# Last batch of a fused attention and convolution kernel: inverse transform interleaved with the previous batch's output projection, and one output DMA per chunk of 128 rows

## The chip, the cores and the metric

One NeuronCore of one Trainium2 chip runs the whole program. The metric is the device time of one execution in microseconds (us). Most executions of one kernel agree within about 1% here. Ratios in this document are the mean time of one kernel's fast runs over the mean time of the other's fast runs of the same rounds on the same chip, so they are not quite the ratios of the medians that are quoted beside them. An interval in brackets is a 95% interval. Some executions fall in a slower state; on one core, as here, a run counts as slow when it is over 1.5% above the fastest of its kernel.

A "profile" is one execution recorded by the hardware profiler. It gives each instruction's start and length, what it waited for, and each DMA packet. The engines are PE (TensorE), DVE (VectorE), ACT (ScalarE), POOL (GpSimd) and SP (SyncE). SyncE computes nothing here; it issues output DMAs. "SPq" and "ACTq" are the instructions with which SyncE and ScalarE issue a DMA; an issue goes to the queue of its engine. A matmul leaves its result in a PSUM tile, and an "eviction" is the copy from there to SBUF by ScalarE or VectorE, from where a DMA stores it.

## The reference

For 8 batches of 8 heads, 576 positions and 64 channels:

```python
kv  = einsum('bhsd,bhse->bhde', k, v)
out = einsum('bhsd,bhde->bhse', q, kv)
x   = rms_norm(out) * g_norm            # to (8, 576, 512)
x1, x2, x3 = split(x @ w_proj)          # 512 columns each
y   = x1 * irfft(rfft(x2) * rfft(filter)) * x3      # over the 576 positions
return y @ w_out                        # float32, (8, 576, 512)
```

The output of one batch is 576 rows of 512 float32, 1.18 MB.

## The kernel before

The batches are software-pipelined. While batch b's gates and transforms run, batch b+1's attention runs beside them, and batch b-1's output projection (`outp`) is done just before batch b's inverse transform. Only the last batch has nothing to overlap with, so it has a routine of its own, `last`.

The rows come out in nine blocks of 64. Block x holds rows 192*(x//3) + x%3 + 3*i, for i = 0..63. So rows of one block lie three rows apart in memory, and 128 consecutive columns of `yg` (one chunk) are two such blocks.

```python
def o_rows(b, *blks):
    t0 = [SB * (x // 3) + x % 3 for x in blks]
    two = [[(t0[1] - t0[0]) * DM, 2]] if len(t0) == 2 else []
    return bass.AP(..., offset=out.offset + (b * S + t0[0]) * DM, ap=[[3 * DM, 64]] + two + [[1, DM]])

def inv(b, dcs):                        # one quarter (dc) of the inverse
    ...                                 # 6 matmuls of 288 columns into PSUM
    nc.scalar.copy(out=os_, in_=p_[1])  # os has one buffer
    nc.vector.tensor_add(out=u[...], in0=p_[0], in1=os_)
    nc.vector.tensor_sub(out=u[...], in0=p_[0][...], in1=os_[...])
    nc.vector.tensor_mul(out=st[b]['yg'][:, d2], in0=u, in1=g13[:, d2])

def last(b):
    po = [ps_tile("ps_out") for _ in range(3)]
    def part(dc):                       # the share of one dc in all five chunks
        for c in range(4):
            nc.tensor.matmul(po[c // 2][:, c % 2], st[b]['yg'][:, dc, c * P:(c + 1) * P], wo[:, dc], **kw)
        for i, y in enumerate((yt[0], st[b]['yg'])):   # block 8 of batches b-1 and b
            nc.tensor.matmul(po[2][64 * i:64 * i + 64, 0], y[:, dc, 4 * P:S], wo[:, dc], **kw)
    for dc in range(NDC):
        inv(b, (dc,))
        if dc:
            part(dc - 1)
    part(NDC - 1)
    for c in range(NSC):                # evict and store, chunk by chunk
        ...
        if c % 2:
            nc.vector.tensor_copy(out=ot[:, 0], in_=src)
        else:
            nc.scalar.copy(out=ot[:, 0], in_=src)
        for i in range(2):              # two DMAs of 64 rows, two queues
            bb, blk = (b, 2 * c + i) if c < 4 else (b - 1 + i, NR - 1)
            (nc.scalar if i else nc.sync).dma_start(out=o_rows(bb, blk), in_=ot[64 * i:64 * i + 64, 0])

# the loop's end, batch b
if b:
    for c0 in (0, 2, 4):
        outp(b - 1, c0)                 # all of batch b-1's projection first
if not nxt:
    last(b)
```

Of the kernel before, what the change touches and what calls it, by code (L numbers as in the profile page):

```python
# [9 lines left out]
FP32 = mybir.dt.float32  # L10
# [5 lines left out]
P = 128  # L16
# [4 lines left out]
def kernel(  # L21
# [16 lines left out]
    nc = tc.nc  # L38
    B, H, S, D = q.shape
    DM = H * D  # L40
    D3 = 3 * DM
    assert (B, H, S, D) == (8, 8, 576, 64)
    SB = S // 3
    TH = S // 2
    NDC = DM // P
    NSC = 5
# [6 lines left out]
    work = ctx.enter_context(tc.tile_pool(name="work", bufs=1))  # L53
    psp = ctx.enter_context(tc.tile_pool(name="psp", bufs=4, space=bass.MemoryType.PSUM))

    def ps_tile(name):
        return psp.tile([P, 2, 512], FP32, name=name, tag="ps")
# [4 lines left out]
    NR = S // 64  # L62
# [63 lines left out]
    wo = consts.tile([P, NDC, DM], BF16)  # L126
# [14 lines left out]
    for r0, n, a, na, base, step in ((0, 64, 0, 2, 0, 2), (64, 64, 0, 2, 1, SB - 1), (0, 32, 2, 1, SB + 1, 1)):  # L141
        nc.gpsimd.dma_start(out=fa[r0:r0 + n, a:a + na], in_=bass.AP(
            tensor=moe_filter_fft.tensor, offset=moe_filter_fft.offset + base * DM,
            ap=[[3 * DM, n], [step * DM, na], [1, DM]]))
# [20 lines left out]
    for c, tag in enumerate(("x", "Y", "g13")):  # L165
# [15 lines left out]
        tensor=g_norm.tensor, offset=g_norm.offset, ap=[[0, 2], [1, D]]))  # L181
# [31 lines left out]
    x_t, st = {}, {}  # L213
# [82 lines left out]
    def fold(b, jp):  # L296
        s = st[b]
        if jp == 0:
            s['ab'] = work.tile([P, NDC, 2 * SB], BF16, name="ab", tag="ab")
            s['rr'] = work.tile([P, NDC, SB], BF16, name="rr", tag="rr")  # L300
        j2 = slice(2 * jp, 2 * jp + 2)
        x3 = s['x'][:, j2].rearrange("p j (m r) -> p j m r", m=3)
        d_ = work.tile([P, 2, 2, SB], BF16, name="d_", tag="d_")
        nc.vector.tensor_sub(out=d_, in0=x3[:, :, 0:3:2], in1=x3[:, :, 1:2].to_broadcast([P, 2, 2, SB]))
        t_ = work.tile([P, 2, SB], BF16, name="x01", tag="x01")
        nc.vector.tensor_add(out=t_, in0=x3[:, :, 0], in1=x3[:, :, 2])
        r_ = work.tile([P, 2, SB], BF16, name="x012", tag="x012")
        nc.vector.tensor_add(out=r_, in0=t_, in1=x3[:, :, 1])
        hb = SB // 2
        for half, op in ((0, nc.vector.tensor_add), (1, nc.vector.tensor_sub)):  # L310
            op(out=s['rr'][:, j2, half * hb:(half + 1) * hb], in0=r_[:, :, 0:hb], in1=r_[:, :, SB - 1:hb - 1:-1])
            op(out=s['ab'][:, j2, half * SB:(half + 1) * SB], in0=d_[:, :, 0], in1=d_[:, :, 1, ::-1])  # L312
# [127 lines left out]
    def inv(b, dcs):  # L440

        Y, g13 = st[b]['Y'], st[b]['g13']
        if dcs[0] == 0:
            st[b]['yg'] = work.tile([P, NDC, S], BF16, name="yg", tag="yg", bufs=3)
        m = len(dcs)
        if m == 2:
            po, pe = ps_tile("ps_invo"), ps_tile("ps_inve")
            p_ = (pe[:, :, 0:TH], po[:, :, 0:TH])
        else:
            pp = ps_tile("ps_inv")  # L450
            p_ = (pp[:, 0:1, 0:TH], pp[:, 1:2, 0:TH])
        for h in (1, 0):
            for i, dc in enumerate(dcs):
                for g in range(3):
                    n = N1 if g == 0 else P
                    nc.tensor.matmul(p_[h][:, i], Y[:n, 2 * g + h, dc * P:(dc + 1) * P], IV[:n, 2 * g + h],  # L456
                                     start=(g == 0), stop=(g == 2))
        os_ = work.tile([P, 2, TH], FP32, name="os", tag="os")[:, 0:m]
        nc.scalar.copy(out=os_, in_=p_[1])  # L459
        u = work.tile([P, 2, S], BF16, name="u", tag="u", bufs=2)[:, 0:m]  # L460
        nc.vector.tensor_add(out=u[:, :, 0:TH], in0=p_[0], in1=os_)
        nc.vector.tensor_sub(out=u[:, :, TH:S], in0=p_[0][:, :, ::-1], in1=os_[:, :, ::-1])  # L462
        d2 = slice(dcs[0], dcs[0] + m)
        nc.vector.tensor_mul(out=st[b]['yg'][:, d2], in0=u, in1=g13[:, d2])

    yt = {}

    def o_rows(b, *blks):
        t0 = [SB * (x // 3) + x % 3 for x in blks]
        two = [[(t0[1] - t0[0]) * DM, 2]] if len(t0) == 2 else []  # L470
        return bass.AP(tensor=out.tensor, offset=out.offset + (b * S + t0[0]) * DM, ap=[[3 * DM, 64]] + two + [[1, DM]])

    def outp(b, c0):
        if c0 < 4 or b % 2:
            yg = yt[b % 2] = st[b]['yg']
            pp = ps_tile("ps_out")
            if c0 < 4:
                for cc in range(2):
                    c = c0 + cc
                    for dc in range(NDC):  # L480
                        nc.tensor.matmul(pp[:, cc], yg[:, dc, c * P:(c + 1) * P], wo[:, dc], start=(dc == 0), stop=(dc == NDC - 1))  # L481
            else:
                for dc in range(NDC):
                    for i in range(2):
                        nc.tensor.matmul(pp[64 * i:64 * i + 64, 0], yt[i][:, dc, 4 * P:S], wo[:, dc],
                                         start=(dc == 0), stop=(dc == NDC - 1))
            ot = work.tile([P, 2, DM], FP32, name="ot", tag="ot", bufs=3)
            n = 2 if c0 < 4 else 1
            if c0 == 0:
                nc.vector.tensor_copy(out=ot, in_=pp)  # L490
            else:
                nc.scalar.copy(out=ot[:, 0:n], in_=pp[:, 0:n])  # L492
            for i in range(2):
                if n == 2:
                    nc.sync.dma_start(out=o_rows(b, 2 * c0 + i, 2 * c0 + 2 + i), in_=ot[64 * i:64 * i + 64])
                else:
                    nc.sync.dma_start(out=o_rows(b - 1 + i, NR - 1), in_=ot[64 * i:64 * i + 64, 0])

    def last(b):

        po = [ps_tile("ps_out") for _ in range(3)]

        def part(dc):
            kw = dict(start=(dc == 0), stop=(dc == NDC - 1))
            for c in range(4):
                nc.tensor.matmul(po[c // 2][:, c % 2], st[b]['yg'][:, dc, c * P:(c + 1) * P], wo[:, dc], **kw)
            for i, y in enumerate((yt[0], st[b]['yg'])):
                nc.tensor.matmul(po[2][64 * i:64 * i + 64, 0], y[:, dc, 4 * P:S], wo[:, dc], **kw)

        for dc in range(NDC):  # L510
            inv(b, (dc,))
            if dc:
                part(dc - 1)
        part(NDC - 1)
        for c in range(NSC):
            ot = work.tile([P, 2, DM], FP32, name="ot", tag="ot", bufs=3) if c < 3 else \
                work.tile([P, 2, 2, DM], FP32, name="ot_", tag="tpw", bufs=2)[:, 0]
            src = po[c // 2][:, c % 2]
            if c % 2:
                nc.vector.tensor_copy(out=ot[:, 0], in_=src)  # L520
            else:
                nc.scalar.copy(out=ot[:, 0], in_=src)
            for i in range(2):
                bb, blk = (b, 2 * c + i) if c < 4 else (b - 1 + i, NR - 1)
                (nc.scalar if i else nc.sync).dma_start(out=o_rows(bb, blk), in_=ot[64 * i:64 * i + 64, 0])


    qtr(0)
# [9 lines left out]
    for b in range(B):  # L538
        nxt = b + 1 < B
        proj2(b)  # L540
        if b == 0:
            fold_filter()
            proj13(0, 0)
            proj13(0, 1)
            gen_h(1)
            gen_h(0)
            qtr(1)
            gen_h(2)
            kv(1)
        elif nxt:  # L550
            kv(b + 1)
            qtr(b + 1)
        if b + 2 < B:
            load_kv(b + 2, (0, 8))
            load_q(b + 2)
        if b == 0:
            att_o(1, 0)
            fft(0, 1)
            att_o(1, 1)
            att_r(1, 0)  # L560
            fft(0, 0)
            att_r(1, 1)
            att_x(1, 0)
            fold(1, 0)
            att_o(1, 2)
            proj13(0, 2)
            att_o(1, 3)
            att_r(1, 2)
            fft(0, 2)
            att_r(1, 3)  # L570
            att_x(1, 1)
            fold(1, 1)
            proj13(0, 3)
        for dc in range(NDC) if b else ():
            if dc < 3:
                fft(b, (1, 0, 2)[dc])
            if nxt:
                att_o(b + 1, dc)
            proj13(b, dc)
            if nxt:  # L580
                att_r(b + 1, dc)
                if dc % 2:
                    att_x(b + 1, dc // 2)
                    fold(b + 1, dc // 2)
        if b:
            for c0 in (0, 2, 4):
                outp(b - 1, c0)
            del st[b - 1]
        if not nxt:
            last(b)  # L590
            continue
        for dp in (0, 2):
            inv(b, (dp, dp + 1))

# [29 lines left out]
```

## Time and profile before

| what | value | from |
|---|---|---|
| time, median of the first three runs | 255.63 us (254.88 to 257.65) | runs |
| span of the profiled run | 252.9 us (that run took 255.09) | profile |
| PE busy over the span | 88% | profile, part 1 |
| end of the last gate projection (L432) | 230.90 us | chain of waits |
| last eviction ends | 249.09 us | timeline |
| span ends, counted from the last gate projection | 22.0 us | 252.9 - 230.9 |

From run to run the point where the last gate projection ends moves by some 2 us either way, though the program up to there is the same. The stretch after it, the **tail**, repeats far better: in the three kernels with the old order (before, e2, e11) the first eviction starts 13.26 us into it each time. So from here on I count times in profiles from the end of the last gate projection. In the chain of waits of the kernel before, that is the end of this piece (start, length, what):

```profile
226.87 4.03 PE ps_x L432 x32
```

A second view cuts the tail into stretches. Its columns are the stretch, its length, then for PE, PE's weight loads, DVE, ACT and POOL the busy us and instruction count, then the granted clock, the mean busy share of the 16 DMA engines, and the GB/s:

```profile
230.90:240.90 10.00, 8.73 (x50) 4.15 (x48) 5.57 (x11) 2.11 (x4) 0.00 (x0) 1.00 0.37 105
240.90:245.00 4.10, 3.31 (x17) 1.26 (x15) 1.76 (x5) 0.99 (x2) 0.00 (x0) 1.00 0.00 0
245.00:253.00 8.00, 0.00 (x0) 0.00 (x0) 1.16 (x2) 1.17 (x2) 0.00 (x0) 0.64 0.57 164
```

In the first 10 us PE idles for 1.3 us, and in the last 8 us it does nothing at all: there the output is evicted and stored.

### The profile page before, as it was taken

What the parts mean: (1) busy time and instruction counts of PE and PEld (TensorE: products, weight loads), DVE (VectorE), ACT (ScalarE), POOL (GpSimd) and SP (SyncE); (2) the same over time, 40 slices, a digit from 0 to 9 for tenths busy, and PEclk for the clock granted to TensorE, in tenths of its full rate; (3) what the DMA queues carried; (4) which work ended last, traced back from release to release, by engine and by line L of the source; (5) the groups of instructions that cost most, each with busy time, mean ns of one, the idle gap of its engine ahead of it and who ended that gap; (6) DMA issues with size and microseconds to landing.
All of it is one profiled execution on the core that took longest, in us unless ns stands there. A gap on an engine that the chain in (4) does not pass through costs nothing.

```text
span 252.9 us, 4825 instructions
## 1 busy us (share of the span) xinstructions
PE 222.7 (88%) x1927; PEld 132.3 (52%) x1927; DVE 195.1 (77%) x354; ACT 153.3 (61%) x230; POOL 89.7 (35%) x101
## 2 busy tenths in 40 slices
PE   0377997787999999999999999999999999999760
PEld 0343453453665566655665566547664765466420
DVE  6669747799797969795998699769987997696441
ACT  2764336991689468945894689566956696522311
POOL 7964970670491049102920292003300330042000
PEclk9999999999999999999999999999999999999995
DMA  6999999993297529752994199420023003400506
GB/s 69 167 202 251 202 196 191 193 136 43 19 180 85 158 26 181 87 160 54 160 119 115 56 162 118 117 95 1 0 66 103 3 0 75 135 0 3 166 20 187
DMA packets 45623, 27.17 MB, mean 107 GB/s; under 512 B 22274, under 2 KB 40706, under 8 KB 45602
## 3 DMA queue, kind: packets, MB, share of 16 engines
q0 software_dynamic: 40160, 17.44, 55.1%
q1 hardware_dynamic: 5042, 8.78, 12.2%
q10 hardware_dynamic: 400, 0.66, 0.7%
q8 instruction: 15, 0.25, 0.4%
q14 instruction: 6, 0.05, 0.1%
HBM read 33.69 MB, written 9.44 MB: 171 GB/s over the span
## 4 chain that ended last, share of the span: by engine, by line
PE 69%; ACT 13%; DVE 9%; issue 3%; DMA 2%; POOL 2%; ACTq 1%; POOLq 0%; DVEq 0%
PE ps_x L432 19%; PE ps_out L481 10%; PE ps_x L383 6%; PE ps_invo L456 4%; PE ps_inve L456 4%; PE ps_qT L248 3%; ACT lr L284 3%; PE ps_x L389 3%; PE ps_x L374 3%; PE ps_r L283 2%; ACT osb L272 2%; ACT sq L267 2%; DMA vm<-in_v_dram 2%; PE ps_kv L223 2%; PE ps_o L266 2%
## 5 line engine op out<-in xcount | busy, mean ns | idle before, releaser
L432 PE MATMUL ps_x<-x,wp 128*128 128x288 bf16 x512 | 67.8, 286 | 0.7
L415 POOL TENSOR_TENSOR Y<-tpw 128x1024 bf16<-128x1024 f32 (+1 forms) x16 | 37.9, 2366 | 66.3 <-PE ps_r L283 40.7
L432 PEld LDWEIGHTS <-wp 128*128 128x128 bf16 x512 | 49.7, 98 | 15.5 <-issue 2.9
L70 POOL DMA_DIRECT2D km<-in_k_dram x9 | 7.9, 878 | 64.4 <-PE ps_qT L248 58.4
L267 ACT ACTIVATE sq<-ps_o 128x576 bf16<-128x576 f32 x32 | 20.7, 653 | 13.4 <-PE ps_o L266 13.4
L438 DVE TENSOR_TENSOR g<-ps_x,x 128x576 bf16<-128x576 f32 x32 | 24.0, 751 | 5.3 <-PE ps_x L432 3.5
L284 ACT ACTIVATE lr<-ps_r,bias_eps 128x576 f32<-128x576 f32 x32 | 23.5, 751 | 6.9 <-PE ps_r L283 6.9
L436 ACT CAST x<-ps_x 128x576 bf16<-128x576 f32 x32 | 20.7, 648 | 8.4 <-PE ps_x L432 8.4
L481 PE MATMUL ps_out<-wo,yg 128*128 128x512 bf16 x112 | 25.3, 379 | 0.0
L253 DVE COPY qT<-ps_qT 128x512 bf16<-128x512 bf16 (+1 forms) x32 | 13.4, 453 | 14.7 <-PE ps_qT L248 14.6
L456 PEld LDWEIGHTS <-Y 128*128 128x128 bf16 (+1 forms) x192 | 18.2, 97 | 9.2 <-DVE Y L421 1.8
L413 DVE TENSOR_TENSOR tpw<-ps_X,HH 128x1024 f32<-128x1024 f32 (+1 forms) x16 | 19.5, 1219 | 3.9 <-PE ps_X L411 3.3
L272 ACT ACTIVATE osb<-ps_o,g_col 128x576 bf16<-128x576 f32 x28 | 20.9, 746 | 0.0
L248 PE MATMUL ps_qT<-ident,qb 128*64 128x128 bf16 x288 | 12.3, 232 | 9.3 <-DMA qb<-in_q_dram 8.7
L459 ACT COPY os<-ps_invo 128x576 f32<-128x576 f32 x14 | 9.0, 640 | 18.0 <-DVE u L462 15.3
L414 DVE TENSOR_TENSOR tpw<-ps_X,HH 128x1024 f32<-128x1024 f32 (+1 forms) x16 | 19.4, 1213 | 0.0
L287 ACT ACTIVATE rstd<-lr 128x1152 bf16<-128x1152 f32 x16 | 18.6, 1164 | 0.4
L383 PE MATMUL ps_x<-wp,ab 128*128 128x512 bf16 x64 | 16.9, 404 | 1.3 <-DVE ab L312 1.3
L481 PEld LDWEIGHTS <-yg 128*128 128x128 bf16 x112 | 11.0, 98 | 11.9
L492 ACT COPY ot<-ps_out 128x1024 f32<-128x1024 f32 (+1 forms) x10 | 8.8, 885 | 12.9 <-PE ps_out L481 12.9
L266 PE MATMUL ps_o<-qT,kvblk 128*128 128x288 bf16 x64 | 13.8, 304 | 2.9 <-ACT kvblk L234 1.9
L248 PEld LDWEIGHTS <-qb 128*64 128x64 bf16 x288 | 9.6, 117 | 12.3 <-issue 12.3
(166 smaller groups left out, 396.6 us busy)
## 6 DMA issues: line engine op xcount, KB each, us to landing
out_dram<-ot SPq DMA_DIRECT2D x28, 256.0 KB, 3.6
qb<-in_q_dram POOLq DMA_DIRECT2D x16, 288.0 KB, 7.0
km<-in_k_dram POOLq DMA_DIRECT2D x7, 512.0 KB, 6.1
vm<-in_v_dram POOLq DMA_DIRECT2D x7, 512.0 KB, 8.2
wp<-in_moe_w_proj_dram POOLq DMA_DIRECT2D x3, 512.0 KB, 10.1
out_dram<-ot SPq DMA_DIRECT2D x9, 128.0 KB, 3.0
km<-in_k_dram POOLq DMA_DIRECT2D x2, 256.0 KB, 5.5
kt<-in_k_dram POOLq DMA_DIRECT2D x8, 64.0 KB, 5.7
```

The lines of the kernel that those rows point to most:

```text
L248: mm = nc.tensor.transpose(tp[64 * hp:64 * hp + 64, bank, i * P:(i + 1) * P], qb[b % 2][:, 2 * jj + hp, c * D:(c + 1) * D], ident)
L267: nc.scalar.activation(out=s['sq'][:, j].rearrange("p (a b) -> p a b", a=2), in_=op[:, :, 0:TH], func=AF.Square)
L272: nc.scalar.activation(out=o_, in_=op[:, :, 0:TH], func=AF.Copy, scale=g_col)
L284: nc.scalar.activation(out=s['lr'][:, j % 2].rearrange("p (a b) -> p a b", a=2), in_=r2[:, :, 0:TH], func=AF.Ln, scale=1.0 / D, bias=bias_eps)
L383: nc.tensor.matmul(pp[:, h], ab[:, j, h * SB:h * SB + P], wp[:, j, DM:2 * DM], start=(j == 0), stop=(j == NDC - 1))
L413: nc.vector.tensor_mul(out=t_[:n, 0], in0=xp[:n], in1=HH[:n, g, 1:3])
L415: nc.gpsimd.tensor_add(out=Y[:n, 2 * g:2 * g + 2], in0=t_[:n, :, 0], in1=t_[:n, :, 1])
L432: nc.tensor.matmul(pp[:, h, 0:TH], w_, x[:, j, h * TH:(h + 1) * TH], start=(j == 0), stop=(j == NDC - 1))
L436: nc.scalar.copy(out=x1, in_=pp[:, :, 0:TH])
L438: nc.vector.tensor_mul(out=st[b]['g13'][:, dc].rearrange("p (a b) -> p a b", a=2), in0=pp[:, :, 0:TH], in1=x1)
L456: nc.tensor.matmul(p_[h][:, i], Y[:n, 2 * g + h, dc * P:(dc + 1) * P], IV[:n, 2 * g + h], start=(g == 0), stop=(g == 2))
L481: nc.tensor.matmul(pp[:, cc], yg[:, dc, c * P:(c + 1) * P], wo[:, dc], start=(dc == 0), stop=(dc == NDC - 1))
```

## The change

The intent is threefold. Batch 6's projection is split in two and laid between the quarters of batch 7's inverse, so that TensorE has work while the other engines prepare `yg`. Each chunk of 128 rows then gets a PSUM tile of its own, and ScalarE and VectorE evict chunks side by side. And each chunk leaves in one DMA of 256 KB on SyncE, where two of 128 KB went out on two queues.

```diff
-    def outp(b, c0):
+    def outp(b, c0, ev=None):
 ...
+    def out1(b, c, ev, q1):
+        yg = st[b]['yg']
+        pp = ps_tile("ps_out")
+        for dc in range(NDC):
+            ...                        # 4 matmuls, or 8 half-width ones for chunk 4
+        ev(out=ot[:, 0], in_=pp[:, 0])
+        t0 = [x * S + SB * (y // 3) + y % 3 for x, y in (((b, 2 * c), (b, 2 * c + 1)) if c < 4 else ((b - 1, NR - 1), (b, NR - 1)))]
+        q1.dma_start(out=bass.AP(tensor=out.tensor, offset=out.offset + t0[0] * DM,
+                                 ap=[[(t0[1] - t0[0]) * DM, 2], [3 * DM, 64], [1, DM]]), in_=ot[:, 0])
+
     def last(b):
-        po = [ps_tile("ps_out") for _ in range(3)]
-        ...                            # part() and the evictions, above
         for dc in range(NDC):
             inv(b, (dc,))
-            if dc:
-                part(dc - 1)
+            if dc < 2:
+                outp(b - 1, 2 * dc, nc.scalar.copy)
+        act, dve = nc.scalar.copy, nc.vector.tensor_copy
+        for c, ev in ((4, act), (0, dve), (1, act), (2, act), (3, dve)):
+            out1(b, c, ev, nc.sync)
 ...
+        if not nxt:
+            last(b)
+            continue
         if b:
             for c0 in (0, 2, 4):
                 outp(b - 1, c0)
             del st[b - 1]
-        if not nxt:
-            last(b)
-            continue
```

The store's destination is two blocks of 64 rows of 512, with 2 outermost.

## The prediction

> **What bounds the kernel now.** I read the page first: PE is busy 88% of the span, so the body of the kernel is TensorE's. The change leaves the body alone: the comparison of instruction orders shows the same 3856 TensorE rows, and differences only after the last gate projection (L432). So what counts is the last 22 us, and there I read the chain of waits from 230 us on, pieces with start, length and what ran.
>
> ```profile
> 230.90 3.47 PE ps_out L481 x16
> 234.39 1.01 ACT ot L492
> ...
> 243.00 0.47 DVE yg L464
> 243.47 0.05 issue
> 243.52 0.62 PE ps_out L506 x2
> 244.14 0.02 issue
> 244.16 0.59 ACT ot L522
> 244.76 0.02 issue
> 244.78 0.70 DVE ot L520
> 245.48 0.02 issue
> 245.50 0.69 ACTq L525
> ```
>
> Three stretches are to be seen. TensorE first does batch 6's whole output projection (16 matmuls, 3.47 us) ahead of the last inverse. Then the inverse runs a ladder: a copy on ScalarE, two VectorE operations, the product yg, with TensorE waiting; the last yg ends at 243.47. Then five evictions pass ScalarE and VectorE one after the other, because ScalarE also issues DMAs that wait for VectorE's copy (the "ACTq" piece); the last eviction ends at 249.09, and 3.8 us later the span ends, with its last DMA. Next come the DMA view of the last 8.4 us, and that of the first 12 us, where SyncE's queue q1 carries only the load of g_col:
>
> ```profile
> DMA packets 800, 1.31 MB, mean 156 GB/s; under 512 B 160, under 2 KB 160, under 8 KB 800
> q1 hardware_dynamic: 400, 0.66, 32.3%
> q10 hardware_dynamic: 400, 0.66, 22.3%
> ```
>
> ```profile
> q1 hardware_dynamic: 130, 0.00, 0.5%
> ```
>
> The last batch leaves as ten DMAs of 64 rows: 640 packets of 2 KB and 160 small ones, 16 for each DMA. The small ones are the completions, one from each of 16 engines. But g_col's load (128 elements of 4 bytes, its source described as 2 x 64) made 130 packets: 128 plus **two** completions. It ran on two engines. For this change that is the weightiest line of the profile.
>
> **What the Trainium skill says.** "DMA: Bandwidth & Descriptors", section "Why a DMA increments its semaphore by 16 and not by 1": a DMA's engine count is the largest number up to 16 that divides the size of the slowest dimension of both its access patterns, and only those engines write a completion. The trace agrees: 160 completions for ten DMAs with 64 outermost, 2 for the one with 2 outermost. The same page, "Rules for kernel authors": an outermost dimension under 16 confines the whole DMA to at most that many engines. The same page, "Specifications": some 27 GiB/s for each engine. The trace's shortest 2 KB packets take 81 to 84 ns, 24 GB/s, a little less. The same page, "Issuing engines are not separate DMA queues": SyncE and ScalarE share the engines, so moving all issues to SyncE costs issue time only; the old tail fits, with q1 and q10 moving equal bytes in one stretch.
>
> **The change part by part.** *Interleaving.* Counts stay: 24 inverse matmuls of some 0.123 us (6 take 0.74 on the chain), 16 of batch 6 and 16 of batch 7 at 0.216 (3.47/16), and 8 half-width ones that pair up to about 1.1 us: 2.96 + 3.45 + 3.45 + 1.1 = 11.0 us. Before, they lie between 230.9 and 244.9, 14 us, so up to 3 us of TensorE waiting can go. I step the ladder through the new order: inverse 0 at 230.75, half of the projection at 231.5, inverse 1 at 233.2, the other half at 234.0, inverses 2 and 3 at 235.7 and 236.45. ScalarE starts a copy about 1.0 us after its inverse starts, VectorE's product ends 1.75 later. ScalarE's two 1.01 us copies of batch 6 fall between, and the fourth copy waits for the one buffer os, freed at about 238.1. The last yg is then ready at 240.0, 3.5 us earlier. After it nine matmuls are left, 1.95 us: the last ends near 242.1.
>
> *Evictions.* Each chunk now has its own PSUM tile, and ScalarE (three, 0.59 us) and VectorE (two, 0.69 us) work side by side, without DMA issues on ScalarE. They end at about 241.0, 241.35, 241.6, 242.2 and 242.9: the last one 6.2 us before the old last.
>
> *Issues.* Ten of about 0.5 us on two queues become five of 0.6 to 0.9 us on SyncE (batch 5's output shows 613 ns for one of 256 KB, 913 behind others). The first is at about 241.05, against 244.77.
>
> *Transfers.* This decides. The diff writes the destination as [2][64][512], outermost 2; the built program keeps that form for all five. By g_col's 130 packets each should run on two engines, 64 packets of 2 KB on each. The five queue up: 320 packets an engine. One takes 84 ns where an engine always has descriptors waiting, and some 150 where a lone DMA starts. In the last 8.4 us q10 shows 22.3% x 16 x 8.4 / 320 = 94 ns a packet and q1 136. With a full backlog on two uncontended engines I choose 90 ns, so 28.8 us, an estimate. Data started 1.25 us after the first issue in batch 5's output (211.76 to 213.0), so here at 242.3, and ends at 271.1. From the last data (251.45) to the span's end lay 1.45 us before: span 272.55. The median time stands 2.7 us over the profiled span (255.63 against 252.9): **275.3**, say 275.5 us. Of that, 3.7 us is gained by the earlier first issue, and some 23 us is lost, as old data flowed for 5.5 us (245.95 to 251.45) and the new for 28.8.
>
> **The rivals.** *All 16 engines are used.* For it: the source side is 128 partitions, and all of the kernel's other output DMAs spread. Against: g_col's destination too is 128 partitions and only its source is 2, and it spread over two. Then five DMAs of 256 KB would flow like batch 5's output, the same 1.31 MB on SyncE alone, some 7.0 us from first issue to last landing. From 241.05 that lands at 248.0, the span ends near 249.2 and the time is 251.5 to 252: 1.5% faster, called the same. *The full gain as well:* if those transfers flow at the 350 GB/s of the best stretches (1.31 MB in 3.75 us from 242.3), the end is near 247.5 and the time 250.2, just over 2% faster. *The new order stalls*, because ScalarE's copies of batch 6 delay the ladder, or TensorE waits for a PSUM tile of the pool's four: the third chunk's slot hangs on the last inverse, the last chunk's on ScalarE's first eviction, both met within 0.1 us in my stepping. It would cost 1 to 2 us, hidden behind transfers this long only so far as the first issue stays early. *Two engines, but slow packets:* at 150 ns, 48 us and a time near 294; at 27 GiB/s, 22.6 us and 269.
>
> **Range and chances.** The lower end, 268, is the skill's rate for an engine with the earlier issue; the upper, 292, is packets near 145 ns or a stall in the middle. I hold slower for 0.93 likely, since one DMA of this very profile shows the rule; 0.04 for the same, the 16-engine rival; 0.03 for faster.
>
> **What would show it.** In the changed profile: q1's small packets in the last stretch are 2 for each of the five DMAs (10, against 160); the busy share of the DMA engines sits near 2/16, about 0.1, for over 20 us after the last eviction; GB/s is 45 to 50; landing of the five grows from about 6 us to over 25 with each one queued; evictions end near 243, TensorE is done at 242. If instead the small packets are 80 and GB/s is over 200, the central step is wrong, and the rest of my steps give 251.5. If first issue is not near 241, the stepping of the ladder is wrong. If two engines are seen but 120 ns or more a packet, only the size is.

## The result, and the profile after

The changed kernel took 272.2 us (median of 4 runs, 271.0 to 272.73), the kernel before 255.25 us with a further run counted. The ratio of fast runs is 1.0645 [1.0558, 1.0732]: slower by 6.5%.

First the chain of waits after, from the last gate projection on (start, length, what):

```profile
226.07 4.03 PE ps_x L432 x32
230.09 0.74 PE ps_inv L456 x6
...
231.10 1.46 PE ps_out L481 x6
232.56 0.74 PE ps_inv L456 x6
233.31 1.73 PE ps_out L481 x8
235.03 1.49 PE ps_inv L456 x12
...
240.27 1.47 PE ps_out L506 x6
...
241.83 0.69 DVE ot__3271 L512
```

The interleaving works: inverse and projection alternate on PE with hardly a gap, and the chain no longer passes through ScalarE and VectorE until the last eviction, which ends at 242.52. That is 12.4 us after the last gate projection, where the kernel before needed 18.2. The stretches say the same (columns as above):

```profile
230.10:240.10 10.00, 9.95 (x56) 4.90 (x57) 5.88 (x13) 3.55 (x7) 0.00 (x0) 1.00 0.41 105
240.10:243.00 2.90, 1.58 (x7) 0.54 (x6) 1.38 (x2) 1.44 (x3) 0.00 (x0) 1.00 0.06 11
243.00:270.00 27.00, 0.00 (x0) 0.00 (x0) 0.00 (x0) 0.00 (x0) 0.00 (x0) 0.55 0.12 47
```

PE is busy for 9.95 of the first 10 us, against 8.73. Then come 27 us in which no engine computes and the DMA engines are busy to 0.12 of the 16. The clock of 0.55 there is PE's, which has nothing to do, so it explains nothing.

The DMA view of the last 30 us, in 40 slices: busy share in tenths, GB/s, packets, then the only queue with traffic:

```profile
DMA  0001111111111111111111111111111111111100
GB/s 0 0 16 27 22 41 46 55 49 49 55 49 52 52 49 52 52 49 55 49 49 55 49 52 52 49 52 52 49 55 49 49 55 49 52 52 49 55 5 0
DMA packets 650, 1.31 MB, mean 44 GB/s; under 512 B 10, under 2 KB 10, under 8 KB 650
q1 hardware_dynamic: 650, 1.31, 11.7%
```

The same 640 packets of 2 KB go out as before, but with 10 small packets for five DMAs, two each, where the ten DMAs before had 160. They flow at a steady 50 GB/s or so. In the trace's packet records the first of the 640 starts at 241.78 and the last ends at 268.67, and the small ones come in pairs 5.12 us apart (248.1, 253.3, 258.4, 263.5, 268.6): one DMA is 64 packets on each of two engines, 80 ns a packet. The packet records do not name the engine, but for 26.8 of the 26.9 us exactly two packets are under way. Lastly the issues (start, length, what):

```profile
240.59 0.55 SPq L514 DMA_DIRECT2D out_dram<-ot__3239  x1
241.24 9.01 SPq L514 DMA_DIRECT2D out_dram<-ot  x3
250.35 4.92 SPq L514 DMA_DIRECT2D out_dram<-ot__3271  x1
```

One issue took 0.55 us at first; of the three in the middle line one took 0.54, the others 3.55 and 4.74, and the last 4.92. SyncE was held while it issued. Is that the cause of the loss or its consequence? It is the first rival below.

### The profile page after: what moved, and what is told of

Same layout as the page of the kernel before. It is cut to its first block, busy times and chain, and to the rows that moved or that the text cites. A ratio compares the mean times of both kernels' runs of the same rounds, so it can differ in the third digit from the quotient of the medians.

```text
span 269.9 us, 4797 instructions
## 1 busy us (share of the span) xinstructions
PE 219.1 (81%) x1903; PEld 132.2 (49%) x1927; DVE 193.9 (72%) x353; ACT 154.2 (57%) x231; POOL 88.1 (33%) x101
## 3 DMA queue, kind: packets, MB, share of 16 engines
q1 hardware_dynamic: 5292, 9.44, 11.9%
## 4 chain that ended last, share of the span: by engine, by line
PE 64%; ACT 10%; DVE 8%; issue 4%; DMA 2%; POOL 2%; POOLq 0%; DVEq 0%; ACTq 0%
PE ps_x L432 17%; PE ps_out L481 9%; PE ps_x L383 5%; PE ps_invo L456 4%; PE ps_inve L456 3%; PE ps_qT L248 3%; ACT lr L284 3%; PE ps_x L389 3%; PE ps_r L283 2%; DMA vm<-in_v_dram 2%; PE ps_x L374 2%; PE ps_o L266 2%; PE ps_kv L223 2%; ACT sq L267 2%; ACT rstd L287 2%
## 5 line engine op out<-in xcount | busy, mean ns | idle before, releaser
L456 PEld LDWEIGHTS <-Y 128*128 128x128 bf16 (+1 forms) x192 | 18.4, 97 | 8.7 <-DVE Y L421 1.6
L414 DVE TENSOR_TENSOR tpw<-ps_X,HH 128x1024 f32<-128x1024 f32 (+1 forms) x16 | 19.4, 1213 | 0.0
L383 PE MATMUL ps_x<-wp,ab 128*128 128x512 bf16 x61 | 15.8, 389 | 1.7 <-DVE ab L312 1.3
L481 PEld LDWEIGHTS <-yg 128*128 128x128 bf16 x112 | 10.9, 98 | 11.7
L492 ACT COPY ot<-ps_out 128x1024 f32<-128x1024 f32 (+1 forms) x11 | 9.8, 896 | 11.6 <-PE ps_out L481 11.6
```

Of the source, the lines that this page charges most:

```text
L383: nc.tensor.matmul(pp[:, h], ab[:, j, h * SB:h * SB + P], wp[:, j, DM:2 * DM], start=(j == 0), stop=(j == NDC - 1))
L456: nc.tensor.matmul(p_[h][:, i], Y[:n, 2 * g + h, dc * P:(dc + 1) * P], IV[:n, 2 * g + h], start=(g == 0), stop=(g == 2))
L481: nc.tensor.matmul(pp[:, cc], yg[:, dc, c * P:(c + 1) * P], wo[:, dc], start=(dc == 0), stop=(dc == NDC - 1))
```

## The experiments

The **main theory**: the number of DMA engines that a DMA runs on is set by the outermost dimension of its destination, here 2, and the loss is the time that two engines need for 320 packets each. The rivals: **A**, one queue is too slow for 1.31 MB because issues block it; **B**, the new order of matmuls and evictions costs the time; **C**, what is slow is a DMA of 128 rows or 256 KB, or the order in which rows go to memory, whatever the outermost size.

Twelve kernels ran. "End" is the span's end in us after the last gate projection, from the profile.

| run | output of the last batch | time, us | ratio to before | end |
|---|---|---|---|---|
| before | ten DMAs of 64 rows, two queues | 255.25 | 1 | 22.0 |
| changed | five of 128 rows, outermost 2, SyncE | 272.2 | 1.0645 | 39.8 |
| e1 | ten of 64 rows, SyncE, changed order | 252.79 | 0.9907 | 19.6 |
| e2 | before's order, five with outermost 2 | 275.68 | 1.0847 | 43.2 |
| e3 | changed, but two queues | 271.83 | 1.0661 | 40.1 |
| e4 | as e1, outermost 4 in nine of ten | 260.33 | 1.0214 | 27.5 |
| e5 | as e1, outermost 8 in nine of ten | 253.12 | 0.9986 | 21.5 |
| e6 | five of 256 KB with outermost 128 or 64 | 250.18 | 0.9832 | 17.9 |
| e7 | as e1, but two queues | 251.56 | 0.9851 | 17.9 |
| e8 | as e1, last chunk with outermost 2 | 256.57 | 1.0096 | 24.5 |
| e9 | as e6, but two queues | 250.13 | 0.9844 | 18.4 |
| e10 | as e6, without interleaving | 250.96 | 0.9879 | 19.1 |
| e11 | before, all ten DMAs on SyncE | 255.85 | 1.0053 | 23.0 |
| e12 | as e1, first chunk with outermost 2 | 254.31 | 0.9995 | 22.1 |

Ratios belong to the rounds of their own run: the kernel before stood at 255.15 to 255.18 us in the rounds of e1 to e8, and at 253.98 us, on another chip, in those of e9 to e12.

The profiled runs of e1 and e9 fell in the slow state. The times are medians of all runs, and no difference below rests on those two profiles alone: e11's, a fast one, has the same 6.5 us of data as e1's. In e1's, the 2 to 4 us were lost before the tail began (the last gate projection ended at 233.33); its first eviction starts 9.88 us into the tail, as in the changed kernel (9.88).

### e1: each chunk as two DMAs of 64 rows

```diff
-        q1.dma_start(out=bass.AP(..., ap=[[(t0[1] - t0[0]) * DM, 2], [3 * DM, 64], [1, DM]]), in_=ot[:, 0])
+        for i, (x, y) in enumerate(...):         # the chunk's two blocks
+            q1.dma_start(out=bass.AP(..., ap=[[3 * DM, 64], [1, DM]]), in_=ot[64 * i:64 * i + 64, 0])
```

> The changed kernel with one thing undone: each chunk of 128 rows leaves as two DMAs of 64 rows (64 outermost), still all on SyncE. Main theory (the engine count of a DMA is set by its outermost dimension, 2 before, 16 here): ten DMAs with 16 completions each, data flows for 5 to 6 us from about 1.2 us after the first issue, and the span ends some 8.7 us after the first issue: 251 to 252.5 us, ratio to the kernel before 0.98 to 0.99. Rival A (a single SyncE queue is too slow for 1.31 MB, because issues block it): the time stays well above 260, since all is on that one queue here too. Rival B (the new order of matmuls and evictions costs time): the time stays above the kernel before.

Correct, 252.79 us, ratio 0.9907 [0.9836, 0.9977], a little above what was expected of it. All 19.4 us of the loss (272.2 - 252.8) go with this one edit. Order of matmuls, evictions, bytes, rows and queue are those of the changed kernel, so rival B falls, and A falls as far as one queue in itself is concerned. The DMA view of the tail:

```profile
GB/s 142 212 243 162 212 192 213 212 192 172 263 182 182 263 192 172 213 253 172 182 212 233 182 223 202 182 212 202 223 202 182 172 20 0 0 0 0 0 0 0
DMA packets 800, 1.31 MB, mean 162 GB/s; under 512 B 160, under 2 KB 160, under 8 KB 800
```

160 completions are back, and with them some 200 GB/s. But 200 is flat, and no bin passes 263, while the kernel before had bins of 400 with the same DMAs on two queues. So a second limit shows here, one that the prediction did not have: about 100 packets in a us (640 in 6.5 us). The issues tell what it is:

```profile
243.82 1.13 SPq L515 DMA_DIRECT2D out_dram<-ot__3239  x2
245.05 3.74 SPq L515 DMA_DIRECT2D out_dram<-ot  x6
248.89 1.19 SPq L515 DMA_DIRECT2D out_dram<-ot__3275  x2
```

Ten issues of 0.49 to 0.60 us follow one another for 6.3 us, and by the packet records about 128 KB, one DMA, land from the end of one issue to the end of the next. The first two issues took 0.49 and 0.60 us with no data under way yet, and the others were no longer, so nothing held them up: the output flows at the pace at which one queue issues DMAs of 64 rows. No run changes the time of an issue alone, but e6 (half as many issues) and e7 (issues on two queues) come back to it.

### e2: the kernel before with the new DMA form alone

```diff
-            for i in range(2):
-                bb, blk = ...
-                (nc.scalar if i else nc.sync).dma_start(out=o_rows(bb, blk), in_=ot[64 * i:64 * i + 64, 0])
+            nc.sync.dma_start(out=bass.AP(..., ap=[[(t0[1] - t0[0]) * DM, 2], [3 * DM, 64], [1, DM]]), in_=ot[:, 0])
```

> The kernel before with only the DMA form of the change: its own order of matmuls, but each chunk of the last batch leaves as one DMA with outermost dimension 2, on SyncE. Main theory: two engines, 320 packets of 2 KB each at 80 ns measured in the changed kernel = 25.6 to 27 us of data from 1.2 us after the first issue at about 244.8; span end near 274, time 275 to 278, ratio 1.075 to 1.09. Rival B (the new order is what costs): ratio near 1.00. If the form is the whole loss, this run is slower than the changed kernel by the 3.4 us by which its first issue is later.

Correct, 275.68 us, ratio 1.0847 [1.0783, 1.0910]. The form alone carries the whole loss onto the old order. Its end, 43.2, is 3.4 us behind the changed kernel's 39.8, by just as much as its first issue is later (13.9 us into the tail against 10.5). That difference is what the rest of the change gained.

Ten completions again in the tail's DMA view:

```profile
DMA packets 650, 1.31 MB, mean 46 GB/s; under 512 B 10, under 2 KB 10, under 8 KB 650
```

### e3: two queues, outermost still 2

```diff
-        for c, ev in ((4, act), (0, dve), (1, act), (2, act), (3, dve)):
-            out1(b, c, ev, nc.sync)
+        for c, ev, q1 in ((4, act, nc.sync), (0, dve, nc.scalar), (1, act, nc.sync), (2, act, nc.scalar), (3, dve, nc.sync)):
+            ...                                  # ScalarE's two issued after the others
```

> The changed kernel with its DMA form kept, but two of the five DMAs moved from SyncE's queue to ScalarE's. Main theory: both queues feed the same two engines, so the total per engine stays 320 packets and the time stays at 272 us within 1.5 us. Rival A (the blocked SyncE queue, with issues of up to 4.9 us, is the limit): the three DMAs on SyncE and the two on ScalarE flow side by side, some 16 us of data in place of 27, and the time falls to 260 to 263.

Correct, 271.83 us, ratio 1.0661 [1.0594, 1.0728]: no change. The issues, the last of which was over 21 us before data stopped flowing (270.35 in the packet records), are these, and below them the two queues' packets:

```profile
244.05 5.07 SPq L514 DMA_DIRECT2D out_dram<-ot__3269  x1
244.33 0.54 ACTq L514 DMA_DIRECT2D out_dram<-ot  x1
```

```profile
q1 hardware_dynamic: 390, 0.79, 7.7%
q10 hardware_dynamic: 260, 0.52, 4.7%
```

The second line of the first fence shows an issue of 0.54 us on ScalarE's queue, to the same two engines, at a time when SyncE's took 5.07. So it is not the full engines as such that hold an issue, but, as far as these runs show, the backlog of its own queue: in the changed kernel, e2 and e3, SyncE's first two issues took 0.54 to 0.56 us and its third 3.50 to 5.07. With two queues the last issue was over at 249.1, in the changed kernel only at 255.3, and yet the end is the same (40.1 against 39.8 us into the tail). The held issue is a consequence of the slow output and not its cause; rival A falls altogether. Both queues feed the same two engines.

### e4 and e5: outermost 4 and 8

These write the right rows in the wrong order (wrong results): nine of the ten 64-row DMAs of e1 write k groups of 64/k rows, so that only the outermost size, and the order of rows in memory, differ from e1. The tenth, batch 6's last block, keeps 64 outermost.

```diff
-    ap = [[3 * DM, 64], [1, DM]]                              # e1
+    ap = [[3 * 48 * DM, 4], [3 * DM, 16], [1, DM]]            # e4, k = 4
+    ap = [[3 * 24 * DM, 8], [3 * DM, 8], [1, DM]]             # e5, k = 8
```

> Wrong result on purpose: ten DMAs of 64 rows on SyncE as in the run with 64 outermost, same rows written once each, but nine of them write 4 groups of 16 rows, outermost dimension 4, so that the last batch's rows land in another order. Main theory: 4 completions for each of the nine, four engines with 9*16 + 4 = 148 packets at 80 ns = 11.8 us of data, span end about 14.3 us after the first issue, time 256 to 258.5, ratio 1.00 to 1.013. Rival C (what is slow is one DMA of 128 rows or 256 KB, not its outermost size): as the run with two DMAs of 64 rows, 251 to 252.5.

> Wrong result on purpose, as the run with outermost dimension 4, but nine of the ten DMAs of 64 rows write 8 groups of 8 rows, outermost dimension 8. Main theory, with what the first runs showed: eight engines at 80 ns a packet can take 100 packets in a us, and one queue of 64-row DMAs was seen to deliver no more than about 100 in a us even with 16 engines, so data flows 6.4 to 8 us (9*8 + 4 = 76 packets an engine, 6.1 us, and up to 1.5 us at the start): time 252.5 to 254.5, ratio 0.985 to 1.0, hardly behind the run with 64 outermost. Rival C (not the engine count but the rows' order in memory made the run with 4 slow): it is slower than the run with 4, as its pieces are smaller still, 8 rows.

e4 took 260.33 us, ratio 1.0214 [1.0121, 1.0308]; e5 253.12 us, 0.9986 [0.9888, 1.0084]. The DMA views of their tails, e4 first:

```profile
GB/s 165 180 46 52 62 72 72 46 62 52 72 72 77 93 103 93 103 103 98 103 103 103 103 93 103 103 103 103 103 103 103 98 103 103 98 41 5 0 0 0
DMA packets 692, 1.31 MB, mean 82 GB/s; under 512 B 52, under 2 KB 52, under 8 KB 692
```

```profile
GB/s 174 199 174 108 91 116 207 190 149 215 199 190 149 149 132 124 83 116 108 116 174 182 149 190 182 157 207 182 157 190 199 207 108 25 0 0 0 0 0 0
DMA packets 728, 1.31 MB, mean 132 GB/s; under 512 B 88, under 2 KB 88, under 8 KB 728
```

The small packets count the engines: 52 is 9 times 4 and 16, 88 is 9 times 8 and 16. The steady rate follows: some 50 GB/s with two engines, 103 with four, up to 207 with eight in its best slices, each engine one packet of 2 KB in 80 ns. In the packet records four packets are under way for 12.5 of e4's 14.4 us of data, and eight for 5.7 of e5's 8.4 (6.4 to 8 had been expected). Rival C falls: DMAs of 64 rows and 128 KB are as slow for their engine count, and 8 groups of 8 rows are faster than 4 of 16.

The size for e4 was off. I expected 256 to 258.5 us from 148 packets at 80 ns; data took 2.6 us more (14.4), because for the first 4 to 5 us the four engines moved 46 to 77 GB/s and not 103. The changed kernel starts as slowly (16 to 46 GB/s in its first slices). Within that time some packets take over 200 ns, up to 554. The cause is open.

### e6: one DMA for 128 rows that spreads

Blocks x and x+3 follow each other in memory at the same step of three rows, so 128 rows made of them need one dimension, not two. Chunks become blocks (0,3), (1,4), (2,5); block 6 and 7 share 64 partitions and leave as [64][2], and so do the two blocks 8. A first version that gave the two blocks to one matmul as one operand did not build, so each pair is two half-width matmuls side by side. There are four evictions in place of five, one of them twice as wide.

```diff
-        ap=[[(t0[1] - t0[0]) * DM, 2], [3 * DM, 64], [1, DM]]
+        out=o(b * S + c, [[3 * DM, P], [1, DM]])                         # c = 0, 1, 2: outermost 128
+        out=o(b * S + 2 * SB, [[3 * DM, 64], [DM, 2], [1, DM]])          # blocks 6, 7
+        out=o((b - 1) * S + 2 * SB + 2, [[3 * DM, 64], [S * DM, 2], [1, DM]])   # both blocks 8
```

> The change's aim, one DMA per 128 rows, in a form that spreads: blocks of 64 rows are paired so (0 with 3, 1 with 4, 2 with 5) that 128 rows have one step in memory, and the four blocks left go out as two DMAs of 64 partitions with two rows each. Five DMAs of 256 KB on SyncE, outermost 128 or 64. Main theory: 16 completions each, and data flows like batch 5's output (5.1 us for 1.31 MB on one queue), a us or more faster than ten DMAs of 64 rows: span end 17.5 to 18.8 us after the last gate projection, where ten DMAs gave 19.6 and the kernel before 22.0; time 251 to 252, ratio 0.98 to 0.987. Rival A (large DMAs on one queue block it): 260 or more.

Correct, 250.18 us, ratio 0.9832 [0.9768, 0.9895], the lowest ratio of all (those of e7 and e9 lie within its interval), with a time below the 251 to 252 us that were expected. Five DMAs of 256 KB on one queue, so it is not their size that hurt. The first and the last issue (start, length), then the DMA view from shortly after the first data on:

```profile
240.31 0.35 SPq L518 DMA_DIRECT2D out_dram<-ot  x1
...
242.68 1.28 SPq L518 DMA_DIRECT2D out_dram<-ot__3284  x1
```

```profile
GB/s 389 416 322 349 161 269 161 242 161 81 322 27 229 336 322 295 296 255 255 296 309 282 349 376 403 349 255 175 148 107 81 40 0 0 0 0 0 0 0 0
```

No issue took over 1.28 us, all five were done in 3.7 us, and most slices of the transfer lie over 250 GB/s.

### e7 and e9: a second queue

e7 is e1 with the second half of each chunk on ScalarE's queue; e9 is e6 with two of its five DMAs there.

```diff
-            q1.dma_start(out=..., in_=ot[64 * i:64 * i + 64, 0])         # e1, i = 0, 1
+        nc.sync.dma_start(out=o_rows(*blks[0]), in_=ot[0:64, 0])         # e7
+        later.append(lambda: nc.scalar.dma_start(out=o_rows(*blks[1]), in_=ot[64:P, 0]))
```

> The changed order, each chunk as two DMAs of 64 rows, the first half on SyncE's queue, the second on ScalarE's. Theory (with 16 engines the limit of the last stretch is the rate of some 100 packets in a us that one queue of such DMAs delivers): two queues deliver more, data flows for 4 to 5 us in place of 8.7, span end 16.5 to 18 us after the last gate projection in place of 19.6; time 249.5 to 251.5, ratio 0.975 to 0.985. Rival (the 16 engines themselves or the memory are full at 205 GB/s): no change against the run on one queue, ratio 0.99.

> The form of one DMA per 128 rows that spreads, with two of its five DMAs on ScalarE's queue, issued after the copies that they need. Theory: the last stretch is bound by how soon DMAs are issued and by the rate of one queue, so a second queue shortens it by up to 1 us: span end 16.8 to 17.9 us after the last gate projection against 17.9 with one queue and 22.0 in the kernel before; time 249 to 250.5, ratio 0.975 to 0.984. Rival (the 1.31 MB is bound by engines or memory by now): 17.9 and ratio 0.983 as with one queue.

e7: correct, 251.56 us, ratio 0.9851 [0.9772, 0.9931], end 17.9 against 19.6, at the upper edge of what was expected. e9: correct, 250.13 us, 0.9844 [0.9795, 0.9893], no better than e6 on one queue, which speaks for its rival. e7's tail:

```profile
GB/s 91 260 208 104 182 377 403 403 416 234 312 286 299 260 208 299 273 338 286 325 364 325 273 260 273 286 364 325 247 39 0 0 0 0 0 0 0 0 0 0
```

The 16 engines and the memory took these 64-row DMAs at 283 GB/s on the mean (1.31 MB in 4.63 us) and up to 416; one queue gave 200. On two queues the ten issues were done in 3.6 us, where one took 6.3. So the flat 200 of e1 is a limit of one queue's DMAs of 64 rows, and the time of its issues accounts for it. Larger DMAs on one queue (e6) do not meet it. The busy share of the DMA engines would not have shown it: 0.88 in e1 at 201 GB/s and 0.89 in e7 at 283, because e1's packets are recorded as longer (median 151 ns against 84). Why they are, these runs do not tell.

### e8 and e12: one chunk alone with outermost 2, last or first

```diff
-        for i in range(2): ...                                           # e1
+        if c == 3:                                                       # e8; c == 4 in e12
+            q1.dma_start(out=bass.AP(..., ap=[[(t0[1] - t0[0]) * DM, 2], [3 * DM, 64], [1, DM]]), in_=ot[:, 0])
+        else: ...                                                        # the two halves
```

> As the run with 64-row DMAs on SyncE, but the last chunk alone leaves as one DMA with outermost dimension 2. Main theory: 64 packets on each of two engines, 5.1 us at 80 ns, start when the earlier rows are nearly out, some 16 to 17 us after the last gate projection; data ends at about 21.5 to 23.5 and the span at 23 to 25, so 3 to 5 us later than with halves alone: time 255.5 to 257.5, ratio 1.00 to 1.01. Were the loss not by DMA but by some common cause of all five, this one would cost a fifth of 19 us or nothing; the two-engine reckoning gives nearly the same here, so this run tests only the size.

> As the run with the last chunk alone in the form with outermost dimension 2, but with the first chunk in it in place of the last. Theory: the two engines start their 64 packets 5 us earlier and take their eighth share of the other chunks behind them, 96 packets each, 7.7 us at 80 ns and some 1.5 to 3 us of slow start, from 11.9 us on: data ends at 20 to 22, span at 21.5 to 23.5, against 24.5 with the last chunk so; time 253 to 255.5, ratio 0.99 to 1.00. If a DMA on two engines holds up everything behind it on the queue: at or above the run with the last chunk.

e8: correct, 256.57 us, 1.0096 [1.0015, 1.0177], end 24.5 against 19.6. e12: correct, 254.31 us, 0.9995 [0.9942, 1.0049], end 22.1. Both as expected. The GB/s of the two tails, e8 first:

```profile
GB/s 178 197 210 197 210 197 210 197 210 197 210 203 210 197 210 203 57 13 38 38 25 25 25 38 57 32 51 57 51 51 57 51 51 51 51 13 0 0 0 0
```

```profile
GB/s 15 31 15 46 23 85 8 62 46 70 162 185 186 232 325 186 116 170 240 255 247 209 155 85 240 240 139 232 232 70 240 216 132 46 8 0 0 0 0 0
```

In e8 the last 256 KB trickle at 13 to 57 GB/s with nothing beside them and cost 4.9 us of end. In e12 they come first; others flow beside them later, and the cost is 2.5 us. They do hold up what is behind: the six middle DMAs land 6.9 us after issue (median), in e1 2.3.

### e10: without the interleaving

```diff
-        for dc in range(NDC):
-            inv(b, (dc,))
-            if dc < 2:
-                outp(b - 1, 2 * dc, nc.scalar.copy)
+        for c0 in (0, 2):
+            outp(b - 1, c0)
+        for dc in range(NDC):
+            inv(b, (dc,))
```

> The same five spreading DMAs and evictions, but without the interleaving: batch 6's whole projection first, then the four inverses, then batch 7's projection. Theory: the last yg is ready at some 10.3 us after the last gate projection against 9.0 with interleaving, so first issue and end move by about 1.3 us: end at 19 to 19.5 us, time 251 to 252, ratio 0.987 to 0.993. If interleaving is worth nothing: end at 17.9, ratio 0.983. If it is worth the 3 us of waiting that the old tail showed: end near 21.

Correct, 250.96 us, 0.9879 [0.9839, 0.9919], end 19.1 against e6's 17.9. By the profiles, one of each, the interleaving is worth 1.2 us, as expected, and not the 3 us that TensorE waited in the old tail. The edit also gives the eviction of batch 6's first half back to VectorE, as before. The ratios agree in direction (0.9832 against 0.9879), but they come from two chips and their intervals overlap.

### e11: the old tail with unchained evictions

```diff
-                (nc.scalar if i else nc.sync).dma_start(out=o_rows(bb, blk), ...)
+                nc.sync.dma_start(out=o_rows(bb, blk), ...)
```

> The kernel before with all ten of its last DMAs of 64 rows on SyncE, so that ScalarE issues none and its evictions do not wait for VectorE's. Theory: evictions end some 3 us earlier (about 15 us after the last gate projection against 18.2), and yet the end does not move forward, since ten 64-row DMAs on one queue flow at 100 packets in a us: first data at 15.1, 6.5 us of it, end at 22.5 to 23.3 against 22.0; ratio 1.00 to 1.007. Rival (the chain of evictions sets the end): end at about 19, ratio 0.988.

Correct, 255.85 us, 1.0053 [1.0004, 1.0103], end 23.0 against 22.0. The evictions ended 3 us sooner (15.2 us into the tail against 18.2), and nothing came of it: on one queue the ten DMAs need 6.5 us for their data, so the output drains no sooner. The edit took the second queue away together with the chain of evictions, so it does not show what earlier evictions would be worth with two queues.

```profile
242.51 3.69 SPq L525 DMA_DIRECT2D out_dram<-ot  x6
...
247.58 1.19 SPq L525 DMA_DIRECT2D out_dram<-ot__3273  x2
```

The issues follow one another from 242.51 to 248.77 without a wait for an eviction. What counts in this tail is when the first chunk is issued (13.9 us into it in both) and at what rate the output drains.

## Why the prediction was right

It said slower, 275.5 us, and the time came out at 272.2, inside the range. By its steps, in us after the last gate projection (predicted minus 230.9, measured minus 230.1):

| step | predicted | measured |
|---|---|---|
| last `yg` ready | 9.1 | 9.0 |
| first issue | 10.15 | 10.5 |
| TensorE done | 11.2 | 11.6 |
| last eviction ends | 12.0 | 12.4 |
| first data | 11.4 | 11.7 |
| data flows for | 28.8 | 26.9 |
| last data to span's end | 1.45 | 1.2 |
| span's end | 41.65 | 39.8 |

*The interleaving and the evictions* came out within 0.4 us. The late part is the nine matmuls after the last `yg`, 2.2 us where I had 1.95: chunk 4's half-width matmul is followed by a gap in the weight loads. *The central step*, two engines for each DMA, is shown by the ten small packets and by e1, e2, e4 and e5. It was read from one line of the profile before, 130 packets for a load of 128 elements, which fits the rule that the prediction quotes. So the mechanism was right, and no luck was needed. *The packet's time* was over-sized: I chose 90 ns; engines with a full backlog need 80, and the slow first 3 us bring the mean to 26.9 / 320 = 84. That is 1.9 of the 3.4 us by which the prediction of 275.3 lies above the profiled run's 271.93. Of the rest, 0.8 is the body's drift (230.1 against 230.9), and 0.7 a slip of mine: I added a median time less one run's span (2.7), where the runs' own difference is 2.2 before and 2.0 after.

*The issues* were wrong. I had 0.6 to 0.9 us each; three of the five took 3.5 to 4.9 us. It cost nothing (e3), since the engines were the bound. (The 613 and 913 ns are misread: 614 is the median and 913 the longest of eight issues of batches 5 and 6; batch 5's four took 595 to 876.) *The rival with 16 engines* was put at 251.5 to 252. With the ten smaller DMAs it is 252.8 (e1), with the five large ones 250.2 (e6). What I missed for e1 is that ten issues in a row on one queue take 6.3 us. *Landing times* of over 25 us did not come: the DMA view gives none for these five, but their completions in the packet records lie 7.6, 12.0, 16.5, 18.0 and 18.3 us after the start of their issues. They grow as said, but the late ones were also issued late.

What the change aimed at is worth having: with a store that spreads it gives 1.7% (e6) over the kernel before. Of the 4.1 us in the tail, 1.2 come from the interleaving (e10). The other 2.9 are 2.0 of an earlier first issue (11.9 us into the tail in e10 against 13.9) and 0.9 of a shorter way from there to the end (7.2 against 8.1). The large DMAs are not needed for it: e7's ten of 64 rows on two queues end at the same 17.9.

## What to carry to other kernels

Before merging several stores into one DMA, look at the outermost dimension of both sides, in memory too: if it is small (2, 4 and 8 here), the DMA runs on that few engines, whatever its size and the number of partitions. The count of small packets in a DMA view tells how many engines took part, so a mistake of this kind can be read off before it is made. And at the end of a kernel, count from the first issue: the drain of the output took about 7 us from first issue to end at best here, and on one queue the issues themselves can set its pace (ten in 6.3 us in e1). Evictions that ended 3 us sooner gained nothing there (e11); with two queues that was not tried.

## What the Trainium skill lacked or had wrong

- "DMA: Bandwidth & Descriptors", section "Issuing engines are not separate DMA queues", says that a second issuing engine saves only the sequencer's time of issuing, which is usually small beside the DMA itself. The runs agree that it is this time, but it was not small: ten issues of 64 rows of 2 KB took 6.3 us on one queue for 6.5 us of data, at about 200 GB/s (e1), and 3.6 us on two for 4.6 us, at 283 (e7), with 19.6 against 17.9 us to the end. For DMAs of 256 KB a second queue gained nothing (e9).
- The same page, "Specifications", gives some 27 GiB/s (29 GB/s) for an engine. Two engines with a full backlog wrote 64 packets of 2 KB each in 5.12 us, 25.6 GB/s or 23.8 GiB/s for each; larger packets on so few engines were not tried.
- No page that I read says that an issue waits for the backlog of its own queue ("Perfetto Trace Analysis" has a descriptor buffer that can fill, but not this wait): SyncE's issue grew from 0.55 us to 4.92 in the changed kernel, while ScalarE's, to the same two engines, took 0.54 beside SyncE's 5.07 in e3.
- No page that I read has the slow start of a DMA on few engines: with four, 46 to 77 GB/s for the first 4 to 5 us where 103 followed (e4). Its cause is open.
